# A scan's constant operand moved from SBUF to PSUM bytes, and longer due times for early scatters

## The chip, the cores and the metric

One core of a Trainium2 chip runs the whole program in one launch. The metric is the device time of an execution in microseconds; the kernel before was run three times and its median is 836.9 us. One more execution was profiled, and all rows below come from that one.

## The reference

Three layers run one after the other. The first is a linear attention with a decaying state (4 batches, 8 heads, 768 steps, 48 channels a head), the second sends each of the 3072 tokens to one of 8 experts, the third is a dense layer with a smooth gate.

```python
for t in range(S):                                   # attention, S = 768
    cur = np.einsum('bhd,bhe->bhde', u[None] * kt, vt)
    y[:, :, t] = np.einsum('bhd,bhde->bhe', rt, state + cur)
    state = wt[:, :, :, None] * state + np.einsum('bhd,bhe->bhde', kt, vt)
...
expert_idx = np.argmax(logits, axis=1)               # router, N = 3072, E = 8
for e in range(E):                                   # experts, F = 1024
    mask = expert_idx == e
    h = np.maximum(x[mask] @ w1[e], 0.0)
    out[mask] = gate_w[mask, None] * (h @ w2[e])
...
h = x @ w_in                                         # dense layer, 384 -> 2048 -> 384
sp = np.where(h > 20.0, h, np.log1p(np.exp(np.minimum(h, 20.0))))
out = (h * np.tanh(sp)) @ w_out
```

## The kernel before, in words

The attention is cut into 12 chunks of 64 steps. For a chunk `s`, `scaled` turns the decays `w` into running products inside the chunk. Sixteen sequences (4 batches by 4 pairs of heads) lie behind one another in a row of 16 x 65 = 1040 numbers, the two heads of a pair on the two halves of the partitions. VectorE makes two scans along that row. The first writes `pre`: it multiplies its running value by `w` and adds `once`, a constant that is 1 at the head of each sequence and 0 elsewhere, so that each sequence starts anew. The second runs backwards over the same `w`, with `anew` (the reciprocals of the chunk's whole products) as what is added, and writes `suf`. `kh` is `k` times `suf`, on VectorE; `rh` is `r` times `pre`, on GpSimd (POOL), two halves each.

From these TensorE makes the scores of the chunk (`scores`, L515), the transposed keys and the state that goes to the next chunk (`carried`, L547, L556, L559), and the outputs (`outputs`, L579, L584). POOL masks half of the scores (`affine_select`, L530). Each chunk gives two tiles of 128 tokens. `Router.tile` transposes a tile (L308) and multiplies it with the expert vectors (logits, L313). Tiles are decided in groups of 6, 6, 4, 4, 2 and 2 (`ROUTED`): `decide` finds the expert, ranks the tokens by a product of a triangle with the one-hot rows (`rank`, L360 to L364), and works out each token's row (`desti`, L375). `send` then lets POOL scatter each tile's rows to the experts' lists in HBM with an indirect DMA (L388). The first expert's rows are read back only when all 24 scatters have landed; then come the experts and the dense layer, which are not planned but written out in order.

PSUM has eight banks of 512 fp32 words a partition. Bank 0 (`g.bank`) is kept for the router: logits and ranks of the groups with at least three tiles, the even groups from word 0, the odd ones from word 192, and two words at 460 for a final check (L663). The other seven are handed out by the plan.

The order of the attention's work on each engine is not that of the code. Each step is entered into a `Plan` with an engine, an assumed duration, and what it reads and writes. `order` walks through the steps in simulated time: it takes the engine whose step can start first, and among that engine's steps that could start within 0.02 us of it the one with the longest `way` to the end. That walk fixes the order of instructions on every engine; the real waits are semaphores, which the framework puts in from the buffers that instructions touch.

```python
way[o.n] = o.us + max([self.wait(o, S[q]) + way[q] for q in out[o.n]] + [o.late])
...
t = max(t, at.get(o.eng, 0.0), at.get("port", 0.0) if o.port else 0.0)
...
t, n = min([c for c in can if S[c[1]].eng == eng and c[0] <= t0 + SLACK], key=lambda c: (-way[c[1]], c[1]))
```

Steps marked `port` exclude one another in the plan, whichever engine they are on. Before the change these are both scans, `kh`, and most POOL steps; the POOL steps that only prepare constants at the start are not marked. `late` is a floor for the way that follows a step: 6 us for each chunk still to come, plus 40, for the scores, the same plus 20 for the copies of the outputs, and a flat 7 (`LATE_S`) for a scatter.

Of the kernel before, what the change touches and what calls it, by code (L numbers as in the profile page):

```python
# [10 lines left out]
F32 = mybir.dt.float32  # L11
F32R = mybir.dt.float32r
BF16 = mybir.dt.bfloat16
I32 = mybir.dt.int32
AF = mybir.ActivationFunctionType
ALU = mybir.AluOpType
# [11 lines left out]
NT = N // 128  # L28
XW = DM + 1
KC = DM // 128  # L30
E, F = 8, 1024
# [6 lines left out]
NW, NR, NK, NV, NX = 2, 2, 3, 3, 12  # L38
# [3 lines left out]
SLACK, LATE_S, LATE_F, LATE_O, LATE_A = 0.02, 7.0, 0.0, 20.0, 40.0  # L42
COLS = [slice(0, 64), slice(64, 128)]
REST = 100
SEG = C + 1
NB = B * NP
WIDE = NB * SEG
# [13 lines left out]
class Plan:  # L61
# [13 lines left out]
    def add(self, eng, us, fn, reads=(), writes=(), wake=None, late=0.0, port=None):  # L75
        o = SimpleNamespace(eng=eng, us=us, fn=fn, wake=self.WAKE[eng] if wake is None else wake, need=set(),
                            late=late, port=eng == "pool" if port is None else port, n=len(self.steps), ps=[k for k in {*reads, *writes} if k[0] == "ps"])
        for k in reads:
            if k in self.writer:
                o.need.add(self.writer[k].n)  # L80
        for k in writes:
            o.need.update(p.n for p in self.readers.pop(k, []))
            if k in self.writer:
                o.need.add(self.writer[k].n)
        for k in reads:
            self.readers.setdefault(k, []).append(o)
        for k in writes:
            self.writer[k] = o
        for k in o.ps:
            self.users.setdefault(k, []).append(o)  # L90
        o.need.discard(o.n)
        self.steps.append(o)
        for k in o.ps:

            u = self.users[k][0]
            u.need.update(p for p in o.need if p < u.n)
        return o
# [94 lines left out]
def setup(g, tmp, plan, then):  # L192
# [3 lines left out]
    t = lambda nm, shape, dt=F32: const.tile(shape, dt, name=nm)  # L196
    g.tri, g.ones = t("tri16", [128, 128], BF16), t("ones", [128, 128], BF16)
    g.tiny = t("tiny", [128, 1])
    add("dve", 0.06, lambda: nc.vector.memset(g.tiny, 1e-30), then, ["tiny"])
    g.iota, g.tok = t("iota", [128, NT, E]), t("tok", [128, NT], I32)  # L200
    g.ebase, g.runs = t("ebase", [128, E]), t("runs", [128, len(ROUTED) + 1, E])
    g.oh, g.dest, g.desti = t("oh", [128, NT, E], BF16), t("dest", [128, NT]), t("desti", [128, NT], I32)
    g.posi, g.ids, g.offi = t("posi", [128, NT], I32), t("ids", [128, NT], I32), t("offi", [128, E], I32)
    g.cnt, g.offs_f = t("cnt", [128, E]), t("offs_f", [128, E])
    g.flag, g.flagi = t("flag", [128, 3]), t("flagi", [128, 3], I32)
    g.enT = t("enT", [128, KC, E])
    g.xs = g.dram.tile([E * N, XW], F32, name="xs")
    g.idc = g.dram.tile([N, 1], I32, name="idc")
    ones_f, tri = tmp.tile([128, 128], F32, name="ones_f"), tmp.tile([128, 128], F32, name="tri")
    io = tmp.tile([128, NT, E], I32, name="io")  # L210
    v, p = nc.vector, nc.gpsimd
# [55 lines left out]
def apart(g, key, dma):  # L267

    g.tc.declare_no_dep(dma.ins, group=key, reason="rows of their own")
    g.tc.add_to_no_dep_group(key, dma.ins)  # L270
    g.scatters.setdefault(key, []).append(dma.ins)
# [9 lines left out]
class Router:  # L281
# [44 lines left out]
    def sums(self, qi, G):  # L326

        def at(lo, hi):
            if G < 3:
                return self.plan.bank["ps", "lg", qi][:, lo:hi]  # L330
            return self.g.bank[:, 192 * (qi % 2) + lo:192 * (qi % 2) + hi]
        lg = lambda: at(0, G * E).rearrange("p (t e) -> p t e", e=E)
        rt = lambda: at(64, 64 + (G + 1) * E).rearrange("p (t e) -> p t e", e=E)
        return lg, rt

    def decide(self, qi, j0, G):
# [49 lines left out]
    def send(self, qi, j):  # L386
        g, nc, add = self.g, self.g.nc, self.plan.add
        add("pool", 1.27, lambda: apart(g, "xs", nc.gpsimd.indirect_dma_start(  # L388
            out=g.xs[:, :], out_offset=bass.IndirectOffsetOnAxis(ap=g.desti[:, j:j + 1], axis=0),
            in_=self.xs[:, j % NX], in_offset=None, bounds_check=E * N - 1, oob_is_err=False)),  # L390
            [("x", j % NX), ("gt", j % NX), ("desti", qi), "slots"], [("sent", j)], wake=2.4, late=LATE_S)

    def finish(self):

# [36 lines left out]
def attention(g, ctx):  # L431
# [6 lines left out]
    add = plan.add  # L438
    ring, early = [ctx.enter_context(tc.tile_pool(name=n, bufs=1, side=sd)) for n, sd in (("at0", "left"), ("at1", "right"))]
    v, p, a, pe = nc.vector, nc.gpsimd, nc.scalar, nc.tensor  # L440
    X = ring.tile([128, NX, XW], F32, name="x")
    router = Router(g, ring, plan, ROUTED, X)
    t = lambda nm, shape, n: [ring.tile(shape, F32, name=f"{nm}{i}") for i in range(n)]
# [7 lines left out]
    t = lambda nm, shape, n: [early.tile(shape, F32, name=f"{nm}{i}") for i in range(n)]  # L451
# [2 lines left out]
    PRE, SUF = t("pre", [128, WIDE], 2), t("suf", [128, WIDE + 2], 2)  # L454
    ANEW, junk = t("anew", [128, WIDE + 1], 1)[0], t("junk", [128, NB, C], 1)[0]
    zs = t("zs", [REST, XW], 1)[0]
    once = t("once", [128, WIDE], 1)[0]
    halves = [slice(NB // 2 * i, NB // 2 * (i + 1)) for i in range(2)]
    ROW = [slice(0, 64), slice(64, 128)]
    late = lambda s: TICK * (NCH - s)  # L460
# [16 lines left out]
    def tokens(x, at):  # L477

        return x[:, at:at + WIDE].rearrange("p (n t) -> p n t", t=SEG)[:, :, :C]

    def scaled(s):

        n, nw, nr, nk = s % 2, s % NW, s % NR, s % NK
        w, kw = W[nw], [("w", nw)]
        add("act", 1.36, lambda: a.activation(
            junk, w[:, :WIDE].rearrange("p (n t) -> p n t", t=SEG)[:, :, 1:], AF.Square, bias=bias, accum_out=viol[:, s:s + 1]),
            kw + ["bias"], ["viol"])
        add("dve", 2.31, lambda: v.tensor_tensor_scan(PRE[n], w[:, :WIDE], once, 0.0, ALU.mult, ALU.add),
            kw + ["once"], [("pre", n)], port=True)
        add("dve", 0.25, lambda: v.reciprocal(ANEW[:, SEG::SEG], PRE[n][:, C::SEG]), [("pre", n)], ["anew"])  # L490
        add("act", 0.2, lambda: a.copy(OWN[:, s], PRE[n][:, C::SEG]), [("pre", n)], [("own", s)])
        add("dve", 2.31, lambda: v.tensor_tensor_scan(SUF[n][:, WIDE::-1], w[:, ::-1], ANEW[:, ::-1], 0.0, ALU.mult, ALU.add),
            kw + ["anew"], [("suf", n)], port=True)
        for i, c in enumerate(halves):
            for nm, x, y, z, at, eng in (("r", R, PRE, RH, 0, p), ("k", K, SUF, KH, 2, v)):
                add("dve" if eng is v else "pool", 0.68 if eng is v else 1.19,
                    lambda x=x, y=y, z=z, at=at, c=c, eng=eng: eng.tensor_tensor(z[nk][:, c], x[nr][:, c], tokens(y[n], at)[:, c], op=ALU.mult),
                    [(nm, nr), ("suf" if at else "pre", n)], [(nm + "h", nk, i)], port=True)
# [98 lines left out]


    load("w", 0)
    add("dve", 0.93, lambda: v.memset(once, 0.0), [], ["once"])  # L600
    add("dve", 0.07, lambda: v.memset(once[:, 0::SEG], 1.0), [], ["once"])
    add("pool", 0.95, lambda: p.memset(R[0], 0.0), [], [("r", 0)], port=False)
    add("dve", 0.93, lambda: v.memset(K[0], 0.0), [], [("k", 0)])
    add("pool", 0.95, lambda: p.memset(ANEW, 0.0), [], ["anew"], port=False)
# [20 lines left out]
    for s in range(NCH):  # L625
# [16 lines left out]
        for q in range(2):  # L642
            router.tile(2 * s + q)
    within_range(g, ring, plan, viol, OWN.rearrange("p s n -> p (s n)"))
    router.finish()
    plan.order()


def within_range(g, pool, plan, viol, own):

    nc, add = g.nc, plan.add
    okm = pool.tile([128, 2], F32, name="f_ok")
    ok16 = pool.tile([128, 2], BF16, name="f_ok16")
    ps = g.bank[:, 460:462]
    v = nc.vector
    add("dve", 0.15, lambda: v.tensor_scalar(viol, viol, FAR, None, op0=ALU.is_le), [], ["viol"])
    add("dve", 0.15, lambda: v.tensor_reduce(okm[:, 0:1], viol, axis=AX.X, op=ALU.min), ["viol"], ["ok0"])
    add("dve", 0.3, lambda: v.tensor_tensor(own, own, own, op=ALU.mult), [], [("own", s) for s in range(NCH)])
    add("dve", 0.3, lambda: v.tensor_scalar(own, own, LEAST * LEAST, None, op0=ALU.is_ge), [], [("own", s) for s in range(NCH)])
    add("dve", 0.3, lambda: v.tensor_reduce(okm[:, 1:2], own, axis=AX.X, op=ALU.min), [("own", s) for s in range(NCH)], ["ok1"])  # L660
    add("dve", 0.15, lambda: v.tensor_tensor(ok16, okm[:, 0:1].to_broadcast([128, 2]), okm[:, 1:2].to_broadcast([128, 2]), op=ALU.mult),
        ["ok0", "ok1"], ["ok16"])
    add("pe", 0.1, lambda: nc.tensor.matmul(ps, lhsT=g.ones, rhs=ok16, start=True, stop=True), ["ones", "ok16"], ["okps"])  # L663
    add("dve", 0.15, lambda: v.tensor_scalar(g.flag[:, 0:1], ps[:, 0:1], 127.5, None, op0=ALU.is_lt), ["okps"], ["flag0"])
# [619 lines left out]
```

## Time and profile before

| what | value |
|---|---|
| three runs | 836.5, 836.9, 844.67 us; median 836.9 |
| profiled execution | 835.85 us, span from first to last instruction 834.0 us |
| mean granted TensorE clock | 0.978 |
| busy: TensorE (PE) | 768.0 us, 92% |
| busy: VectorE (DVE) | 649.9 us, 78% |
| busy: ScalarE (ACT) | 486.9 us, 58% |
| busy: GpSimd (POOL) | 410.7 us, 49% |

Busy shares are means over stages of quite different kinds; the attention ends near 171 us and the first expert's products start near 187 us. PEld is TensorE's load of weights, which runs beside its products. An entry in square brackets behind a row is the idle time of the engine just before the row and what ended it.

### The profile page before, as it was taken

How to read it: one execution, taken by the hardware profiler on the slowest of the kernel's cores; microseconds unless marked ns; L12 is line 12 of the kernel's file. 1: busy time of each engine (PE TensorE's matmuls, PEld its weight loads, DVE VectorE, ACT ScalarE, POOL GpSimd, SP SyncE). 2: the span in 40 equal slices, each digit the busy share in tenths (PEclk: the TensorE clock that was granted, in tenths of full speed). 3: DMA queues.
4: the chain of work that ended last, by engine and by line, in shares of the span. 5: the costliest groups of instructions: out<-in, count | busy, mean ns of one | idle time of the engine just before them, and what ended most of it. 6: DMA issues, size and time to landing. Idle time of an engine off the chain costs nothing. (4 is left out here: it accounts for less than half of the span.)

```text
span 834.0 us, 18322 instructions
## 1 busy us (share of the span) xinstructions
PE 768.0 (92%) x7136; PEld 703.7 (84%) x7136; DVE 649.9 (78%) x995; ACT 486.9 (58%) x974; POOL 410.7 (49%) x365
## 2 busy tenths in 40 slices
PE   2579889859999999999999999999999999999993
PEld 2467778748999999999989999999999999999993
DVE  6879879648988988898878777877876876886782
ACT  3546566435566656656556656656656655755651
POOL 8716365546877787766423353334334334334321
PEclk9989999969999999999999999999999999999997
DMA  7765666336767776875200010000001001001001
GB/s 162 193 167 139 165 177 192 122 126 178 182 169 193 208 193 173 202 202 171 59 2 1 1 38 1 1 10 29 1 0 39 1 1 39 0 1 39 1 2 42
DMA packets 62220, 75.50 MB, mean 91 GB/s; under 512 B 9314, under 2 KB 52394, under 8 KB 62122
## 3 DMA queue, kind: packets, MB, share of 16 engines
q1 hardware_dynamic: 58282, 64.75, 29.8%
q0 software_dynamic: 3840, 9.47, 3.2%
q8 instruction: 58, 0.95, 0.5%
q14 instruction: 40, 0.33, 0.1%
HBM read 63.50 MB, written 10.69 MB: 89 GB/s over the span
## 5 line engine op out<-in xcount | busy, mean ns | idle before, releaser
L1085 POOL TENSOR_TENSOR t<-t,t 128x512 f32<-128x512 f32 x94 | 122.0, 1299 | 239.2 <-ACT t L1081 228.0
L1094 DVE TENSOR_TENSOR gl<-t,gh 128x512 fp32r<-128x512 f32 (+1 forms) x97 | 113.6, 1171 | 74.6 <-ACT gh L1091 74.3
L1078 ACT ACTIVATE t<-t,two 128x512 f32<-128x512 f32 (+1 forms) x97 | 69.9, 721 | 118.1 <-DVE t L1075 118.1
L817 PE MATMUL acc<-woh,gl 128*128 128x384 f32 x384 | 129.6, 338 | 0.1
L815 PE MATMUL acc<-woh,gh 128*128 128x384 f32 x384 | 129.3, 337 | 0.0
L816 PE MATMUL acc<-wol,gh 128*128 128x384 f32 x384 | 129.0, 336 | 0.0
L886 POOL TENSOR_TENSOR w0l<-r,w0h 128x384 fp32r<-128x384 f32 x63 | 67.6, 1072 | 60.5 <-ACT w0h L885 49.5
L810 PE MATMUL ph<-xl,wih 128*128 128x512 f32 x240 | 95.0, 396 | 0.0
L809 PE MATMUL ph<-xh,wil 128*128 128x512 f32 x240 | 94.8, 395 | 0.0
L808 PE MATMUL ph<-xh,wih 128*128 128x512 f32 x240 | 93.3, 389 | 0.0
L815 PEld LDWEIGHTS acc<-woh,gh 128*128 128x128 f32 x384 | 72.2, 188 | 4.2
L816 PEld LDWEIGHTS acc<-wol,gh 128*128 128x128 f32 x384 | 72.1, 188 | 4.0
L886 POOL TENSOR_TENSOR w1l<-r,w1h 128x384 fp32r<-128x384 f32 x63 | 71.4, 1134 | 4.4 <-ACT w1h L885 4.1
L817 PEld LDWEIGHTS acc<-woh,gl 128*128 128x128 f32 x384 | 72.0, 188 | 0.4 <-DVE gl L1094 0.4
L1088 DVE TENSOR_TENSOR t<-t,ph 128x512 f32<-128x512 f32 (+1 forms) x97 | 64.9, 669 | 5.8 <-POOL t L1085 5.7
L810 PE MATMUL acc<-hl,w1h 128*128 128x420 f32 x192 | 68.0, 354 | 1.3 <-DVE hl L964 1.3
L808 PE MATMUL acc<-hh,w1h 128*128 128x420 f32 x192 | 69.1, 360 | 0.0
L1091 ACT CAST gh<-t 128x512 fp32r<-128x512 f32 (+1 forms) x97 | 58.9, 607 | 16.9 <-DVE t L1088 16.6
L1068 DVE TENSOR_SCALAR t<-ph 128x512 f32<-128x512 f32 (+1 forms) x97 | 65.4, 675 | 3.4 <-PE ph L810 3.1
L1075 DVE SCALAR_TENSOR_TENSOR t<-t 128x512 f32<-128x512 f32 (+1 forms) x97 | 66.2, 683 | 2.1 <-ACT t L1071 2.1
L809 PE MATMUL acc<-hh,w1l 128*128 128x420 f32 x192 | 67.6, 352 | 0.0
L808 PE MATMUL ph<-xh,w0h 128*128 128x420 f32 x189 | 66.7, 353 | 0.0
(201 smaller groups left out, 1808.3 us busy)
## 6 DMA issues: line engine op xcount, KB each, us to landing
r<-in_moe_w SPq DMA_DIRECT2D x128, 192.0 KB, 3.7
w<-in_w_t SPq DMA_DIRECT2D x12, 520.5 KB, 4.4
d<-in_moe_w_in SPq DMA_DIRECT2D x16, 384.0 KB, 4.0
d<-in_moe_w_out SPq DMA_DIRECT2D x16, 384.0 KB, 4.8
xr<-xs SPq DMA_DIRECT2D x32, 157.9 KB, 4.9
r<-in_r_t SPq DMA_DIRECT2D x24, 192.0 KB, 4.8
k<-in_k_t SPq DMA_DIRECT2D x24, 192.0 KB, 3.8
v<-in_v_t SPq DMA_DIRECT2D x24, 192.0 KB, 3.8
```

What stands on the lines that cost most here:

```text
L808: mm(out, lhsT=wh, rhs=xh, start=start, stop=False)
L809: mm(out, lhsT=wl, rhs=xh, start=False, stop=False)
L810: mm(out, lhsT=wh, rhs=xl, start=False, stop=stop)
L815: mm(out, lhsT=ah, rhs=bh, start=start, stop=False)
L816: mm(out, lhsT=ah, rhs=bl, start=False, stop=False)
L817: mm(out, lhsT=al, rhs=bh, start=False, stop=stop)
L886: (eng or nc.gpsimd).tensor_tensor(lo, r, f32(hi), op=ALU.subtract)
L1068: nc.vector.tensor_scalar(tile_of(i, "t0", mt, bufs=3)[:, q], S[i]["ph"][:, q], 20.0, None, op0=ALU.min)
L1075: nc.vector.scalar_tensor_tensor(t0, t0, 2.0, t0, op0=ALU.add, op1=ALU.mult)
L1078: nc.scalar.activation(tile_of(i, "t1", mt)[:, q], S[i]["t0"][:, q], AF.Ln, bias=g.two)
L1085: (nc.gpsimd if i < TI - 2 else nc.vector).tensor_tensor(t0, t0, S[i]["t1"][:, q], op=ALU.mult)
L1094: nc.vector.tensor_tensor(tile_of(i, "gl", ghl, F32R)[:, q], S[i]["t0"][:, q], f32(S[i]["gh"][:, q]), op=ALU.subtract)
```

## The change

The constant `once` is no longer a row of 1040 fp32 numbers in SBUF. It becomes 1040 bytes in 260 words of PSUM bank 0, from word 212, written at the start as one memset of zeros over the words and four memsets that put a 1 into the right byte of every 65th word. The `pre` scan reads these bytes as its added operand, and its step is no longer marked `port`. To make room, the router's areas in bank 0 move together (104 words a group, ranks from word 48), and the final check's two words go to 208. In the plan the scatter of tile `j` gets a `late` of 7 + 1.3 x (23 - j).

```diff
-            return self.g.bank[:, 192 * (qi % 2) + lo:192 * (qi % 2) + hi]
+            return self.g.bank[:, 104 * (qi % 2) + lo:104 * (qi % 2) + hi]
...
-        rt = lambda: at(64, 64 + (G + 1) * E).rearrange("p (t e) -> p t e", e=E)
+        rt = lambda: at(48, 48 + (G + 1) * E).rearrange("p (t e) -> p t e", e=E)
...
-            [("x", j % NX), ("gt", j % NX), ("desti", qi), "slots"], [("sent", j)], wake=2.4, late=LATE_S)
+            [("x", j % NX), ("gt", j % NX), ("desti", qi), "slots"], [("sent", j)], wake=2.4, late=LATE_S + 1.3 * (NT - 1 - j))
...
-    once = t("once", [128, WIDE], 1)[0]
+    once = g.bank[:, 212:212 + WIDE // 4].bitcast(U8)
...
         add("dve", 2.31, lambda: v.tensor_tensor_scan(PRE[n], w[:, :WIDE], once, 0.0, ALU.mult, ALU.add),
-            kw + ["once"], [("pre", n)], port=True)
+            kw + ["once"], [("pre", n)])
...
-    add("dve", 0.93, lambda: v.memset(once, 0.0), [], ["once"])
-    add("dve", 0.07, lambda: v.memset(once[:, 0::SEG], 1.0), [], ["once"])
+    words = g.bank[:, 212:212 + WIDE // 4].bitcast(I32)
+    add("dve", 0.4, lambda: v.memset(words, 0), [], ["once"])
+    for i in range(4):
+        add("dve", 0.07, lambda i=i: v.memset(words[:, i * (SEG // 4)::SEG], 1 << 8 * i), [], ["once"])
...
-    ps = g.bank[:, 460:462]
+    ps = g.bank[:, 208:210]
```

## Rows read from the trace of the kernel before

**Rows 1.** Busy time by stage: stretch, length, then busy time (instructions) of PE, PEld, DVE, ACT, POOL; clock, DMA.
```profile
13.40:50.00 36.60, 22.45 (x541) 18.93 (x545) 23.93 (x35) 18.51 (x44) 22.34 (x22) 0.95 0.59 152
50.00:171.20 121.20, 105.62 (x3328) 89.51 (x3319) 99.08 (x213) 71.33 (x189) 60.11 (x53) 0.96 0.58 161
...
190.00:834.00 644.00, 628.80 (x3244) 585.45 (x3243) 506.48 (x696) 389.31 (x726) 308.12 (x266) 0.99 0.26 70
```

**Rows 2.** What PE waited for up to 190 us: total us, times, longest us.
```profile
PE bank L547 <- POOL ident masks.py:199: 13.4, 1, 13.4
PE bank L515 <- issue: 10.0, 8, 2.7
...
PE bank L547 <- DVE kh L497: 6.0, 2, 3.7
```

**Rows 3.** Timeline of the attention's end.
```profile
167.96 0.97 POOL L388 DMA_INDIRECT xs<-x,desti  x1 [2.44 <-DVE r_d L348]
...
172.11 0.16 DVE L375 CAST desti<-dest 128x2 int32<-128x2 f32 x1
...
177.20 0.98 POOL L388 DMA_INDIRECT xs<-x,desti  x1 [0.31 <-issue]
...
183.01 1.31 PE L942 MATMUL tr<-ident,xr 105*128 105x105 f32 x6 [6.04 <-ACT xr L800]
```

**Rows 4.** Timeline of the first 20 us: start us, us, engine, line, work.
```profile
3.62 0.23 POOL L610 TENSOR_SCALAR_AFFINE_SELECT same<-same 64x64 f32<-64x64 f32 x1
...
4.54 1.15 ACT L485 ACTIVATE junk<-w,bias 128x1024 f32<-128x1024 f32 x1 [2.43 <-DMA w<-in_w_t]
4.55 2.32 DVE L488 TENSOR_TENSOR_SCAN pre<-w,once 128x1040 f32<-128x1040 f32 x1
4.71 2.20 POOL L612 TENSOR_SCALAR_AFFINE_SELECT after<-after 64x64 f32<-64x64 f32 x1
...
7.27 2.33 DVE L492 TENSOR_TENSOR_SCAN suf<-w,anew 128x1041 f32<-128x1041 f32 x1
7.64 2.00 POOL L610 TENSOR_SCALAR_AFFINE_SELECT same<-same 64x64 f32<-64x64 f32 x1
...
12.02 1.36 POOL masks.py:199 TENSOR_SCALAR_AFFINE_SELECT ident<-ident 128x128 f32<-128x128 f32 x1
...
15.80 2.31 POOL L497 TENSOR_TENSOR rh<-r,pre 128x512 f32<-128x512 f32 x2
...
17.03 2.27 PE L515 MATMUL bank<-rh,kh 64*64 64x64 f32 x64 [1.63 <-POOL rh L497]
...
19.41 0.73 DVE L526 COPY_PREDICATED at<-after,bank 128x512 f32<-128x512 int32 x1 [6.11 <-PE bank L515]
```

**Rows 5.** Timeline, two places where DVE and POOL overlap.
```profile
93.20 0.72 DVE L526 COPY_PREDICATED at<-after,bank 128x512 f32<-128x512 int32 x1
93.25 1.38 POOL L530 TENSOR_SCALAR_AFFINE_SELECT at<-at 64x512 f32<-64x512 f32 x2 [0.73 <-ACT at L528]
...
100.04 2.32 DVE L488 TENSOR_TENSOR_SCAN pre<-w,once 128x1040 f32<-128x1040 f32 x1
...
101.05 2.27 POOL L388 DMA_INDIRECT xs<-x,desti  x1 [6.42 <-DVE desti L375]
```

**Rows 6.** The line of the first scan: ns min/median/max.
```profile
L488 DVE TENSOR_TENSOR_SCAN pre<-w,once x12: 2298/2322/2764, 4.6 to 137.2; 128x1040 f32<-128x1040 f32 x12
```

**Rows 7.** DVE groups by line: shapes, count, busy us, mean ns, idle before them.
```profile
L488 DVE TENSOR_TENSOR_SCAN pre<-w,once 128x1040 f32<-128x1040 f32 x12 | 29.0, 2420 | 0.2
...
L565 DVE TENSOR_TENSOR state<-bank,own 128x384 f32<-128x384 f32 x22 | 11.2, 537 | 5.2 <-PE bank L559 5.2
...
L371 DVE TENSOR_TENSOR runs<-runs,bank 128x8 f32<-128x8 f32 x6 | 0.9, 158 | 3.3 <-PE bank L313 2.2 <-PE bank L663 0.8 <-PE bank L364 0.3
...
L886 DVE TENSOR_TENSOR w0l<-r,w0h 128x384 fp32r<-128x384 f32 x1 | 0.6, 558 | 0.0
```

**Rows 8.** Timeline, a first scan with logits beside it.
```profile
64.29 2.76 DVE L488 TENSOR_TENSOR_SCAN pre<-w,once 128x1040 f32<-128x1040 f32 x1
...
65.45 0.52 PE L313 MATMUL bank<-enT,r_xT 128*64 128x8 f32 x12
```

More of the change, by code (lines that the diff above doesn't have):

```diff
@@ L13 @@
 BF16 = mybir.dt.bfloat16
+U8 = mybir.dt.uint8
 I32 = mybir.dt.int32
```

## The prediction, made before the changed kernel was run

> **What bounds the kernel now.** I read the slices of busy time first, then the busy time by stage, then what PE waits for, and last the timeline of the stretches that the change can touch. The reader should see three different kernels. From 190 us on, PE is busy 628.8 of 644 us [rows 1]: experts and dense layer are bound by TensorE, nothing of the change runs there, and whatever is gained or lost before shifts that part as a whole. Between 50 and 171 us PE is busy 105.6 of 121.2 us, DVE 99.1, POOL 60.1 [rows 1]. Most of PE's 15.6 us of idle time there is no wait for DVE or POOL: the row "issue" of the scores has 10.0 us in 8 pieces [rows 2], which no operand explains. So the steady part is nearly at TensorE's pace. The start is the slack part: between 13.4 and 50 us PE is busy 22.5 of 36.6 us [rows 1], it waits 13.4 us for POOL to make the identity and 6.0 us for `kh` [rows 2]. The end is the other: PE waits 6.0 us before the experts' first transposes [rows 3], behind the last scatter and the read of the experts' rows.
>
> **The scan and POOL.** What the change can remove is a block between two engines. A 64x64 select takes POOL 0.23 us; the same form started at 4.71, inside the first scan of 4.55 to 6.87, takes 2.20 and ends with it [rows 4]. A scatter started inside a `pre` scan takes 2.27 us and ends 0.96 after the scan, where others take 0.97 [rows 3, 5]. Where DVE takes one operand from PSUM there is no such thing: two selects of 64x512 beside a predicated copy from a bank take 0.69 each [rows 5]. So I take it that `pre` with a PSUM operand leaves POOL alone, while `suf` and `kh`, with two SBUF operands, block it as before.
>
> [...]
>
> **Start, step by step.** POOL's eight instructions from 4.71 to 13.38 follow one another with 0.1 us of idle time at most. The select of 4.71 gives back 2.20 - 0.23 = 1.97 us. The next select, at 7.64 for 2.00 us, then starts near 5.7, still beside the scan that no longer blocks, and gives back 1.77 more. The identity's select, now 12.02 to 13.38, falls into the first `suf` scan (7.27 to 9.60) and ends with it, near 9.7. So it comes 3.7 us earlier, and with it what follows on POOL: the three memsets of `v` (2.3 us), and `rh`, now from 15.80 and then from 12.0; its first half, 1.2 us later, releases the scores, now at 17.03 [rows 4]. These release the copy at 19.41, before which DVE sat idle 6.11 us [rows 4]; its queue, and the loads that wait for buffers, go along. I count -3.8 us, at least 0 (loads fill the gap), at most -3.8 for this chain.
>
> **Middle.** The 12 scans have a mean of 2.420 us against a median of 2.322 [rows 6, 7]: three were themselves held by POOL, 1.2 us in all. DVE is busy 82% there and PE 87%, so I count a third, -0.4 us (0 to -1.2). Three scatters and a few selects blocked by `pre` come free sooner; POOL is half idle, so 0.
>
> **The operand's own price.** No row has a byte operand. From both sides by the spread of this scan, 2.298 to 2.764 us [rows 6]: -0.3 to +5.3 us over 12. I take 0, because the nearest pair of rows, 128x384 with one operand from a bank (0.537 us) and with two from SBUF (0.558), shows no surcharge [rows 7], and 2.32 us for 1040 elements is the pace of a recurrence. [...]
>
> **The memsets** at the start (one of 1040 elements out, one of 260 and four small ones in) cost nothing while the load of the first `w` covers them: ACT's first reader waits for it until 4.54 and the scan starts at 4.55 [rows 4]. Without that cover the balance would be about -0.3 us, by the 0.93 and 0.07 us of the plan.
>
> **The longer way of scatters.** By the code a scatter's way was 1.27 + 7 = 8.3; now tile 12 has 22.6, tile 16 has 17.4, tile 22 has 9.6. For tiles 0 to 11 it changes nothing, because their `x` buffer is used again six chunks later and that path is already longer (30 for tile 10 against a new 25). On POOL the rivals, `rh` and the selects, keep longer ways. What moves is the queue before the scatter: turns, logits and ranks of tiles 12 to 23 on PE, decisions on DVE, now ahead of their peers but still behind the outputs, whose way is at least 29. At the end eight scatters stand back to back from 167.96, and the last starts at 177.20, though its `desti` is there at 172.27 [rows 3]. Were POOL free then, the last two would start at 172.3 and 173.6: 3.6 us. I count half, -1.8 (0 to -3.6); what is late next is `desti` itself.
>
> **The wait that is added.** `once` shares bank 0 with logits and ranks. The sum over ranks in L371 waited 2.2 us for a logits product and 0.8 us for L663, both of which write other columns of that bank [rows 7]. So the framework orders all accesses to a bank: a logits product behind a `pre` scan in the order must wait for the scan's end, and behind it stands all of PE's queue; a scan behind logits must wait for PE, and behind it stand `anew`, `suf` and `kh`. The plan doesn't know this, since the keys differ. In today's order one such pair overlaps from 51 us on: logits at 65.45 inside the scan of 64.29 to 67.05, 1.6 us [rows 8]. I count +1.6, from 0 to eight scans of 2.32, 18.6.
>
> **Sum.** -3.8 - 0.4 + 0 - 1.8 + 1.6 = -4.4 us on an execution of 835.85 us (its span of 834.0 and 1.85 around it), so 831.45. The median of the runs is 836.9, 1.05 higher; on that scale 832.5 us, and rivals are given on it too.
>
> **Rivals.** (1) The freed port lets the plan fill DVE's hole. In the plan both scans exclude POOL's `rh`; with `pre` out of that, the second `suf` can be placed before the copy at 19.41, into the 6.1 us of idle time. Then PE's 6.0 us of waits for `kh` go as well: 832.5 - 6.1 = 826.4. For it: PE idles 14 us between 13.4 and 50 [rows 1]. Against: a `suf` there blocks `rh`, which gates the scores. (2) Nothing is gained, or the change doesn't do what it says: bytes from PSUM still block POOL, or the start is held by loads in SP's order and PE's issue gaps, so that PE catches up to the same pace: 837. For it: PE at 87% in the middle. (3) Slower: the bank. If the new order sets logits behind scans, PE stops for up to 2.32 us each time in the stage where it is the bound. Break-even is the gain of 6.0 over 2.32, or 2.6 full waits; five give 11.6 - 6.0 = +5.6, 842.5 us. For it: L371's waits. Against: today one overlap in eight scans.
>
> **How the numbers follow.** Forecast 0.50, (1) 0.20, (2) 0.18, (3) 0.12. About 1%, 8.4 us, is what a measurement here can tell from no change: faster below 828.5, slower above 845.3. Faster gets most of (1) and the forecast's lower edge, 0.24; slower takes half of (3), 0.06; the same 0.70. The forecast alone spans 829 to 836, by its terms' ends. The range reaches to (1) below and into (3) above: 825.5 to 840.5 leaves out about 2 in 10.
>
> **What would show it.** In the changed kernel: POOL's selects near 5 us at 0.23, the identity near 9.7, `rh` before 13 and the scores near 13; `pre` scans at 2.32 with no long POOL partner; the last scatter's start less than 4 us after its `desti`; rows of PE waiting for L488, or of L488 waiting for L313, for the bank. I am wrong if the order changes more than I think: the plan is a chain of close choices, and one product placed elsewhere moves a stage's end by microseconds.

## The result, and the profile of the changed kernel

The changed kernel took 828.5 us (median of four runs, 827.76 to 830.04) beside 837.77 us for the kernel before (four runs): a ratio of 0.988 with a 95% interval of 0.984 to 0.992. The forecast was 832.5 us, -4.4 us; measured were -9.3 us (8.4 below the 836.9 us from which it was made). The time lies inside the range (825.5 to 840.5). The profiled execution has a span of 826.0 us, 8.0 less than before.

Busy time by stage in the changed kernel, in the columns of [rows 1]: the end of the start, the steady part to the last outputs, and the experts with the dense layer.

```profile
13.40:50.00 36.60, 24.99 (x823) 20.86 (x823) 32.09 (x39) 23.47 (x59) 17.88 (x22) 0.91 0.74 170
50.00:163.20 113.20, 97.84 (x3019) 83.39 (x3011) 88.72 (x194) 64.02 (x169) 49.66 (x49) 0.94 0.61 168
...
182.00:826.00 644.00, 628.83 (x3245) 585.48 (x3243) 506.12 (x696) 389.27 (x726) 307.65 (x266) 0.99 0.27 70
```

The last line is the last line of [rows 1] moved by 8 us: nothing in the experts or the dense layer changed, the whole gain lies ahead of 182 us. In the start PE went through 823 products where it had 541 before. Its waits, answering [rows 2]:

```profile
PE bank L548 <- DVE kh L498: 17.4, 3, 11.1
PE bank L516 <- issue: 9.9, 7, 2.3
PE tr L945 <- ACT xr L803: 3.5, 1, 3.5
...
PE bank L361 <- DVE pre L489: 1.1, 1, 1.1
```

The 13.4 us of waiting for the identity are gone; the first wait is now 11.1 us, for `kh`. (Lines of the changed kernel are one or three higher than before: the scan is L489, the scores L516, the scatter L389.) The timeline of the start, answering [rows 4]:

```profile
4.70 0.23 POOL L615 TENSOR_SCALAR_AFFINE_SELECT after<-after 64x64 f32<-64x64 f32 x1
...
5.06 2.32 DVE L489 TENSOR_TENSOR_SCAN pre<-w,bank 128x1040 f32<-128x1040 f32 x1 [0.96 <-DMA w<-in_w_t]
5.66 0.24 POOL L613 TENSOR_SCALAR_AFFINE_SELECT same<-same 64x64 f32<-64x64 f32 x1
...
7.76 0.29 POOL masks.py:199 TENSOR_SCALAR_AFFINE_SELECT ident<-ident 128x128 f32<-128x128 f32 x1
7.77 2.46 DVE L493 TENSOR_TENSOR_SCAN suf<-w,anew 128x1041 f32<-128x1041 f32 x1
...
10.47 3.12 POOL L498 TENSOR_TENSOR rh<-r,pre 128x512 f32<-128x512 f32 x2
...
13.65 1.60 PE L516 MATMUL bank<-rh,kh 64*64 64x64 f32 x64
...
15.38 2.31 DVE L493 TENSOR_TENSOR_SCAN suf<-w,anew 128x1041 f32<-128x1041 f32 x1
...
17.61 0.70 DVE L527 COPY_PREDICATED at<-after,bank 128x512 f32<-128x512 int32 x1
```

The select of 5.66 lies inside the scan and takes 0.24 us; before, the select inside this scan took 2.20. The scores start at 13.65 instead of 17.03. And the plan has set the second `suf` scan (15.38) ahead of the copy (17.61); before, DVE stood idle there for 6.11 us. The outputs of the first chunk are copied out of PSUM at 29.81 us, before at 34.84; those of the fourth at 62.68 against 75.99 would be a lead of 13 us, but of the last at 160.44 against 165.99: the lead swings, and 5.6 us of it reach the end of the attention. The end, answering [rows 3]:

```profile
166.12 0.17 DVE L376 CAST desti<-dest 128x2 int32<-128x2 f32 x1
...
169.02 1.02 POOL L389 DMA_INDIRECT xs<-x,desti  x1 [0.30 <-issue]
...
175.10 1.31 PE L945 MATMUL tr<-ident,xr 105*128 105x105 f32 x6 [3.46 <-ACT xr L803]
```

The last `desti` is 6.0 us earlier than before. The last scatter follows it by 2.90 us (before 5.09), which makes 8.2, and 7.9 of these are still there at the experts' first transposes.

### The profile page after: what moved, and what is told of

It is laid out like the page before. It is cut to its first block, busy times and chain, and to the rows that moved or that the text cites. A ratio compares the mean times of both kernels' runs of the same rounds, so it can differ in the third digit from the quotient of the medians.

```text
span 826.0 us, 18303 instructions
## 1 busy us (share of the span) xinstructions
PE 766.0 (93%) x7136; PEld 702.0 (85%) x7136; DVE 648.3 (78%) x998; ACT 486.3 (59%) x974; POOL 394.9 (48%) x365
```

## The experiments

The change has three parts that can be set one by one: the operand (bytes in PSUM or floats in SBUF), the mark in the plan (the scan excludes POOL or not), and the scatters' way. Without the mark the plan gives another order of instructions on every engine; without the way, another order on PE, VectorE and ScalarE, and on POOL only where the mark is off too. The operand alone doesn't change the order, since the plan only sees names. All of them keep the router's areas in bank 0 where the changed kernel has them. Where floats stood, the constant was written by one memset and four small ones, so that the plan had the same steps.

```diff
# floats instead of bytes
-    once = g.bank[:, 212:212 + WIDE // 4].bitcast(U8)
+    once = t("once", [128, WIDE], 1)[0]
# the mark as before
-            kw + ["once"], [("pre", n)])
+            kw + ["once"], [("pre", n)], port=True)
# the way as before; steeper
-... late=LATE_S + 1.3 * (NT - 1 - j))
+... late=LATE_S)
+... late=LATE_S + 2.6 * (NT - 1 - j))
```

The runs were made in three groups, each on one chip with runs of the kernel before between them. That kernel took 848.07 us (median of 31) in the first group, 839.26 (24) in the second and 848.15 (29) in the third, on three different chips. All ratios are to it within a group; they are not quotients of the two medians, and differ from these by up to 0.0017. From the experts' first transposes to the end of the span all fourteen traces take 650.2 to 652.6 us, so that kernels and chips differ only in what lies ahead of these.

**First group: each part alone, and the two without the bytes.**

> The order of before on every engine; only the scan's constant is read as bytes from PSUM (the five memsets of the changed kernel with it). Theory A (the prediction's start term): POOL is no longer held by the first scan, the selects near 5 us take 0.23, the identity ends near 9.7 instead of 13.4, and the span falls by about 4 us, to 830 on the profile's scale (834.0 before). Theory B (the gain is the plan's new order, the second suf scan placed ahead of the first copy): without that order the start stays within 1.5 us of before, span 832.5 to 834.5. Rival C (the bank): PE waits for the scan or the scan for PE at more than one place, and the span is 834 or more.

> The scan stays on an SBUF operand, but the plan is told that it leaves POOL alone (port mark taken off), so the order is that of the changed kernel but for the scatters' way. Theory A: the block is still there, POOL's selects near 5 us take 2.2, nothing is gained at the start, span 833 to 835. Theory B: the order alone, with the second suf scan ahead of the first copy, brings the steady part 4 to 5.5 us earlier; span 829 to 830.

> Only the scatters' longer way, with the SBUF operand and the port mark of before. The prediction's tail term: last scatter 1.8 us (0 to 3.6) earlier against its desti, span 832. By the trace of the changed kernel, where the last scatter starts 2.7 us after its desti instead of 4.9: span 2.2 us shorter, 831.8. Rival: turns, logits and ranks moved ahead disturb the attention and eat the gain: 834 or more.

> The changed kernel's order on every engine, with the scan's constant as 1040 floats in SBUF. Theory A: without the freed POOL the 4 us at the start are lost again: span 830 against 826.0 of the changed kernel. Theory B: the order carries the gain; span within 1 us of 826, or below it, since the wait for bank 0 (1.1 us once) is gone too.

| kernel | median, us | ratio | 95% interval |
|---|---|---|---|
| bytes alone | 848.33 | 1.0018 | 0.9991 to 1.0044 |
| mark alone | 850.86 | 1.0036 | 1.0009 to 1.0063 |
| way alone | 847.07 | 0.9989 | 0.9966 to 1.0012 |
| mark and way, floats | 849.92 | 1.0023 | 0.9995 to 1.0051 |

No part alone gained, and the mark and the way with floats together gained nothing either. Theory B failed on this chip: the mark's order with floats is 2.8 us slower than before. The way alone shortens the stretch from the last `desti` to the last scatter as forecast (2.92 us, 5.09 before), but nothing of that can be told in the time. Expectations of absolute spans (830, 834) could not be read here, since this chip is 10 us slower. For the bytes alone, theory A's mechanism shows in the trace and no gain can be told from the times: the first outputs come at 32.2 us (34.84 in the first trace of before, 36.07 in the one below), and the outputs that before has at 97.65 and 97.97 come at 91.94. At the next chunk the lead is gone: 113.65, before 112.23 and 113.51. Busy time by stretch and the wait of PE in between:

```profile
92.00:100.00 8.00, 4.91 (x199) 3.84 (x201) 7.71 (x16) 4.36 (x13) 3.44 (x4) 1.00 0.68 200
100.00:111.00 11.00, 10.58 (x124) 7.92 (x115) 1.06 (x3) 5.12 (x12) 6.24 (x7) 0.54 0.39 114
111.00:114.00 3.00, 3.00 (x120) 2.92 (x119) 2.53 (x8) 0.35 (x1) 0.00 (x0) 1.00 0.18 66
...
99.47 1.00 PE L516 MATMUL bank<-rh,kh 64*64 64x64 f32 x33 [3.09 <-issue]
```

PE stood 3.09 us without a product, and then the granted clock was 0.54 for 11 us: PE is busy 10.58 of 11 us, and from 100 to 110 us each stretch of 2 us has a clock of 0.50. Before has its own wait there (1.94 us) and a clock of 1.00 behind it in the trace of the second group:

```profile
104.64 0.82 PE L515 MATMUL bank<-rh,kh 64*64 64x64 f32 x33 [1.94 <-issue]
...
106.00:111.00 5.00, 4.92 (x104) 3.84 (x105) 0.63 (x3) 4.44 (x12) 4.03 (x5) 1.00 0.75 213
```

This does not show that the low clock took the gain. Both traces of before are from faster chips, and against the second of them the bytes lead again at the eighth outputs (127.28, before 130.97) and at the eleventh (162.08 and 165.09); only at the last are they behind (174.53 and 170.64). What before does at that place on a chip like this one was not traced.

**Second group: the whole, and two parts of three.**

> The changed kernel as it is, on the chip of these runs, where the kernel before takes about 848 us rather than 837. Theory D (the parts need one another: the new order pays only with a scan that leaves POOL alone): 0.988 of before again, since each part alone gave 0.999 to 1.004 and order and way without the bytes 1.002. Rival E (the gain hangs on where TensorE's clock falls, which differs by chip): 0.995 to 1.003 here.

> Bytes in PSUM and the mark taken off, scatters with the flat way of before. Theory D: the order of the attention is nearly that of the changed kernel; only the tail term of about 2 us goes, 0.990 to 0.991 of before. Rival (the longer way carries more, by the order it gives the router's work): 0.995 or more.

> Bytes in PSUM and the scatters' longer way, with the plan still told that the scan excludes POOL. Theory D: without the new order no more than the two parts alone, 1.0018 and 0.9989, so 0.998 to 1.003 of before. Rival (bytes pay with any order, and the way pays at the tail): 0.993 or less.

> The kernel before, unchanged, for its profile on the chip of these runs: ratio 0.998 to 1.002. Against its first profile (span 834.0) it shows which stretches are longer here: by rival E the ones with a low granted clock, between 100 and 190 us; by theory D all stretches alike.

| kernel | median, us | ratio | 95% interval |
|---|---|---|---|
| changed kernel | 830.2 | 0.9900 | 0.9862 to 0.9937 |
| bytes and mark | 832.79 | 0.9940 | 0.9911 to 0.9969 |
| bytes and way | 834.26 | 0.9944 | 0.9922 to 0.9966 |
| before | 840.24 | 1.0012 | 0.9981 to 1.0043 |

The gain repeats, as theory D had it for the whole. For the parts it is off: bytes with either of the other two give about 0.6%, more than it allowed for bytes and way (0.998 to 1.003) and less than for bytes and mark (0.990). This chip is one of the faster ones, so that rival E could not be decided here. On it the bytes pay in the order of before too: with the way, which shortens nothing at the end there (4.19 us from the last `desti` to the last scatter, 4.05 and 3.94 in the two traces of bytes alone), they gain 5.0 us. Floats in the new order were not run on a chip like this one, so how the 9.1 us divide between the operand and the order is not shown. Between the changed kernel and the one without the longer way there are 2.6 us of medians, but the intervals overlap, and the traces warn against giving them to the way. The order on PE is the same in both up to the logits that the changed kernel runs near 130 us; yet the outputs ahead of these stand, in the changed kernel and in the one without the way, at

```profile
126.53 0.86 ACT L595 COPY x<-bank 128x384 f32<-128x384 f32 x2
```
```profile
130.67 0.86 ACT L595 COPY x<-bank 128x384 f32<-128x384 f32 x2
```

4.1 us apart before any engine's order on this path differs. Single traces differ by that much. What the way itself does stands at the end: the last scatter starts 2.90 us after the last `desti` with it (167.15 to 170.05) and 4.23 without (170.21 to 174.44), 1.3 us.

**Third group: the operand at equal order, and a steeper way.**

> The changed kernel's order with floats in SBUF, a second time, now beside the changed kernel itself. In the trace of its first run the identity ended at 13.5 instead of 9.5, the first copy stood at 21.60 instead of 17.57, and a POOL product beside the second-chunk scan took 4.33 us for two instead of 2.30. Theory A (bytes carry the gain by what POOL no longer waits for, 4 to 5 us at the start): 0.995 to 1.003 of before, at least 4 us above the changed kernel. Theory B (the order carries it): within 1.5 us of the changed kernel.

> Bytes alone in the order of before, a second time. In its first trace the first outputs were copied at 32.2 instead of 34.8 to 36.1, and the lead of 3 to 6 us held to 92 us and was lost by 114 in a stretch in which the granted clock was 0.50. Theory A on a chip whose clock holds there: 0.995 to 0.997 of before. Rival E (the lead is always given back in low clock): 0.999 to 1.002.

> The changed kernel beside the two runs above. If the kernel before takes 836 to 841 us on this chip: 0.988 to 0.991. If it takes about 848 (the chip of the first four runs): by theory A with rival E, 0.990 to 1.000, and in any case 4 us or more below the same order with floats.

> The changed kernel with twice the slope in the scatters' way (7 + 2.6 us for each later tile), so that the router's work of tiles 0 to 11 is moved ahead as well. By the prediction's account of the way (the last scatters find POOL free) the queue of scatters at the end is shorter still, last scatter 2 us after its desti instead of 2.8: 1 us below the changed kernel. Rival (router work ahead of its need disturbs the attention while it fills): 1 to 4 us above it.

| kernel | median, us | ratio | 95% interval |
|---|---|---|---|
| mark and way, floats | 850.0 | 1.0031 | 1.0009 to 1.0054 |
| bytes alone | 846.75 | 0.9982 | 0.9951 to 1.0013 |
| changed kernel | 846.34 | 0.9983 | 0.9961 to 1.0004 |
| changed, steeper way | 841.83 | 0.9915 | 0.9882 to 0.9948 |

The first and third line have the same order on every engine; only the operand differs. It is worth 850.0 - 846.34 = 3.7 us by the medians (4.1 by the means), about the 4 us that theory A asked for; theory B, within 1.5 us of the changed kernel, is out on this chip. The start with floats:

```profile
4.71 2.12 POOL L615 TENSOR_SCALAR_AFFINE_SELECT after<-after 64x64 f32<-64x64 f32 x1
...
15.89 2.28 PE L516 MATMUL bank<-rh,kh 64*64 64x64 f32 x64 [1.63 <-POOL rh L498]
...
20.45 4.33 POOL L498 TENSOR_TENSOR rh<-r,pre 128x512 f32<-128x512 f32 x2
20.90 2.90 DVE L489 TENSOR_TENSOR_SCAN pre<-w,once 128x1040 f32<-128x1040 f32 x1
...
32.96 0.87 ACT L595 COPY x<-bank 128x384 f32<-128x384 f32 x2 [0.74 <-PE bank L585]
```

and with bytes:

```profile
4.70 0.23 POOL L615 TENSOR_SCALAR_AFFINE_SELECT after<-after 64x64 f32<-64x64 f32 x1
...
13.50 2.27 PE L516 MATMUL bank<-rh,kh 64*64 64x64 f32 x64 [0.93 <-POOL rh L498]
...
18.05 2.30 POOL L498 TENSOR_TENSOR rh<-r,pre 128x512 f32<-128x512 f32 x2
18.50 2.30 DVE L489 TENSOR_TENSOR_SCAN pre<-w,bank 128x1040 f32<-128x1040 f32 x1
...
29.70 0.87 ACT L595 COPY x<-bank 128x384 f32<-128x384 f32 x2 [0.73 <-PE bank L585]
```

With the mark off, the plan lays `rh` beside the scan. With floats each holds the other: 4.33 and 2.90 us; with bytes 2.30 and 2.30. The lead of 3.3 us at the first outputs is 3.3 us at the experts' first transposes as well, with floats and with bytes at

```profile
196.71 1.14 PE L945 MATMUL tr<-ident,xr 105*128 105x105 f32 x6 [3.45 <-ACT xr L803]
```
```profile
193.43 1.31 PE L945 MATMUL tr<-ident,xr 105*128 105x105 f32 x6 [4.38 <-ACT xr L803]
```

though it doesn't stay so in between: at the eighth chunk's outputs it is 6.0 us (123.22 and 117.19). POOL is busy 418.9 us with floats and 398.8 with bytes.

Against before, however, the changed kernel gains only 1.8 us on this chip, inside what rival E gave for a chip like it (0.995 to 1.003) and far from the 0.988 to 0.990 of the faster ones. Its interval (0.9961 to 1.0004) does not exclude that it gains nothing. The bytes alone, at 0.9982, lie between what theory A and rival E expected, and decide nothing. The steeper way gains 4.5 us more, and its interval doesn't touch that of the changed kernel: it is faster than both expectations had it, on the one chip on which it ran. Its last scatter starts 2.23 us after its `desti` instead of 2.93, a gain of 0.7 where 0.8 was expected; the other 3.8 us are not explained by that.

```profile
179.82 0.17 DVE L376 CAST desti<-dest 128x2 int32<-128x2 f32 x1
...
182.05 1.21 POOL L389 DMA_INDIRECT xs<-x,desti  x1 [0.30 <-issue]
```

Where the changed kernel loses on this chip, its own traces tell. Its median is 16.1 us above that of the second group, while before loses 8.9 us from one chip to the other. Busy time from 100 us to the experts' first transposes, first in the second group and then in the third:

```profile
100.00:176.11 76.11, 63.53 (x1809) 54.59 (x1801) 54.38 (x167) 38.91 (x107) 37.47 (x37) 0.92 0.53 157
```
```profile
100.00:193.43 93.43, 72.65 (x1837) 62.03 (x1836) 56.44 (x169) 42.47 (x114) 40.79 (x40) 0.85 0.45 132
...
DVE runs L372 <- remote: 5.1, 1, 5.1
DVE r_mx L348 <- remote: 3.9, 1, 3.9
```

Nearly the same products (1809 and 1837) take PE 9.1 us more at a lower clock (0.85 beside 0.92), and its idle time grows from 12.6 to 20.8 us. Two rows of what DVE waited for are new: 9.0 us that end by "remote", which is what the trace says where it sees nothing on this core that ended them. PE stands behind the second of them: it waits 3.9 us for the one-hot rows. Yet both stalls lead back to PE. The instructions that wait so in this trace (L372, L348 and, on ACT, L317) all read banks that PE's products write, and by the record the products had ended well before. The last ones into the bank that L372 reads, ahead of the first stall's end, are logits that ended at 138.48, and the transposes that ACT waits for beside the second ended at 176.85. That is 5.6 and 2.9 us before the waits end:

```profile
137.20 1.28 PE L314 MATMUL bank<-enT,r_xT 128*64 128x8 f32 x36 [0.66 <-ACT r_xT L317]
144.09 0.16 DVE L372 TENSOR_TENSOR runs<-runs,bank 128x8 f32<-128x8 f32 x1 [5.14 <-remote]
...
176.00 0.85 PE L309 MATMUL bank<-ident,x 128*128 128x128 f32 x6 [0.81 <-DVE x L595]
179.77 0.86 ACT L317 COPY r_xT<-bank 128x384 f32<-128x384 f32 x2 [2.55 <-remote]
```

So by the record these waits outlast the products they are for; why they do, no run shows.

## Why the prediction came out as it did

**Start: -3.8 forecast, -3.3 measured at equal order.** The chain went as worked out: selects at 0.23, the identity at 8.05 to 9.84 in the traces with bytes (forecast 9.7), `rh` from 10.5 to 12.3 (before 13), the scores from 13.2 to 13.7 (near 13). At the first outputs the operand alone gives 3.3 us (third group). The profiled execution has 5.0 us there; the floats in the new order stand at 32.96, 1.9 earlier than before, so that the order seems to have a part in it. The 3.7 us by which the runs of the third group differ are more than this term: they hold all that the operand does, for which start, middle and bank were to give 3.8 + 0.4 - 1.6 = 2.6, and in an order that lays `rh` beside a scan. The forecast let the lead run through to the end; it does at equal order (3.3 us at both ends), while the bytes alone in the order of before showed no gain on the slower chips (0.9982 and 1.0018).

**Rival 1: its mechanism came, its price didn't.** The second `suf` went into DVE's hole, as the rival said, but PE still waits 5.9 us for `kh` in the second chunk, and only the identity's wait went. On a slower chip the mark without bytes costs 0.36%, so there the new order doesn't pay with a scan that holds POOL. With bytes it may be worth up to 4.1 us (834.26 against 830.2 in the second group, with intervals that overlap); in the third group, bytes with the mark and the way are no better than bytes alone (846.34 and 846.75). So it lies between 0 and 4 us.

**Middle: -0.4.** The scans that POOL held are gone (their mean fell from 2420 to 2305 ns, 1.4 us in all; what it gave the whole was not measured by itself), as the one line shows, against a median of 2322 and a longest of 2764 ns [rows 6]:

```profile
L489 DVE TENSOR_TENSOR_SCAN pre<-w,bank x12: 2295/2304/2321, 5.1 to 125.0; 128x1040 f32<-128x1040 f32 x12
```

The same line settles **the operand's own price**, taken as 0: with the byte operand from PSUM the scan takes no longer than with floats from SBUF (medians of 2304 and 2322 ns). For the pace of a recurrence the rows have only the two scans, 2.32 us for 1040 elements and 2.33 for 1041 [rows 4]; what sets it, no run shows.

**Scatters' way: -1.8.** The stretch from `desti` to the last scatter shrank by 2.2 us in the profiled pair. By parts: 1.3 us with bytes and mark, 2.2 with floats in the old order (5.09 to 2.92), and nothing with bytes in the old order (3.94 to 4.05 without the way, 4.19 with it). The length of this stretch came out near the forecast for this change, and depends on the order it meets. What it gives the whole is less sure: the way alone gave 0.9989, and the 2.6 us of the second group lie within the noise.

**Scatters beside scans: 0 in the sum.** In the kernel before four of 24 scatters took 2.26 to 2.93 us beside a scan, where others took 0.97; in the changed kernel none does in its first trace (1.27 us at most). Beside a `suf` scan, still with two SBUF operands, a scatter in the third group's changed kernel took 2.84 us and ended 0.8 us after the scan. What in the scatter is held, the trace doesn't tell.

```profile
112.04 2.32 DVE L493 TENSOR_TENSOR_SCAN suf<-w,anew 128x1041 f32<-128x1041 f32 x1
112.33 2.84 POOL L389 DMA_INDIRECT xs<-x,desti  x1 [0.16 <-issue]
```

**The bank's wait: +1.6.** It exists and is smaller. PE's rank product waited once for the scan, which reads the same bank:

```profile
124.98 2.31 DVE L489 TENSOR_TENSOR_SCAN pre<-w,bank 128x1040 f32<-128x1040 f32 x1
...
127.34 0.18 PE L361 MATMUL bank<-oh,tri 128*128 128x48 bf16 x1 [1.07 <-DVE pre L489]
```

1.1 us here, none in the second trace, 0.3 in the third; in these no scan waited for logits. In the other kernels with bytes PE waited 0.8 to 2.0 us for a scan, or not at all, and one scan (bytes and way) 0.4 us for logits: the wait hangs on the order. None comes near the 6.0 us of rival 3, which is out.

**What was off: the size.** In the profiled pair the account closes. The last outputs are 5.6 us earlier where start, middle and bank together were to give 3.8 + 0.4 - 1.6 = 2.6; the router behind them gives 0.4, where nothing was counted; the scatters' queue gives 2.2 instead of 1.8; 0.2 are lost behind it: 8.0 against 4.4. So the term that was mis-sized is the lead that the attention keeps to its end, 5.6 us instead of 2.6. Of the 3.0 us between, 0.5 are the bank's wait (1.1 instead of 1.6) and 1.2 the lead at the first outputs (5.0 instead of 3.8); the other 1.3 arise further on. The new order, which the forecast carried as a rival and not in the sum, is the likeliest source, by the 4.1 us that the mark was worth in the second group; for this pair it is argued and not shown, because floats in the new order did not run on a faster chip. (What is between these 8.0 us and the 9.3 lies between the profiled executions and the medians.)

By its number the result lies nearer to rival 1 (826.4) than to the forecast (832.5), and the range, 15 us wide, would hold the 1.8 us of the third group as well as the 9.3 of the first runs. That the time fell inside it says little for the sum. One row was read too widely, without a price: of the 10.0 us of "issue" before the scores [rows 2], 2.7 lie ahead of 50 us. Between 50 and 171 us they are 7.3, and only with PE's other "issue" rows, 13.0, most of the 15.6.

What the forecast didn't foresee at all is how much the stage behind the start varies. The gain was 9.3 us in the first runs and 9.1 in the second group, but 1.8 in the third. The stalls that end by "remote" and the lower clock are seen there; what causes them is open, and so is why the changed kernel loses more there than before, of which there is no trace from a chip like that. The clock's part is not shown either: from 100 us to the experts' first transposes it is 0.94 and 0.89 in the two traces of before, and 0.85 in this one of the changed kernel.

## What to carry to other kernels

Before a block between two engines is lifted, find the chain that waits behind it: here a quarter-microsecond select that took 2.2 us beside a scan, and with it the identity and the first scores. A planner may be told of a freed resource only when it is free: on a slower chip the mark without the bytes cost 0.36%. Compare parts on one chip: on the faster chip of the second group two of the three parts gave 0.6% and all three 1.0%; on the slower ones the bytes alone and all three together gave 0.2% at most, and only the steeper way 0.85%. A lead at the start counts only as far as the stage behind it holds the pace, so follow it chunk by chunk, and measure on more than one chip.

## What the runs showed of the hardware

- In the third group the scan with floats in SBUF and the product on POOL beside it held each other: two halves of 128x512 took 4.33 us beside the scan with floats and 2.30 beside the one with bytes, and the scan 2.90 and 2.30.
- In the kernel before a memset on POOL was not held: one of 64x768 took 0.73 us inside a scan with two SBUF operands, as another did right behind one.

```profile
6.86 0.73 POOL L621 MEMSET v<- 64x768 f32 x1
...
10.97 2.33 DVE L488 TENSOR_TENSOR_SCAN pre<-w,once 128x1040 f32<-128x1040 f32 x1
11.08 0.73 POOL L621 MEMSET v<- 64x768 f32 x1
```

- The chips differ by about as much as the change is worth: the kernel before took 837 to 839 us in the first runs and the second group, 848 in the first and third. None of the six traces from the former has a DVE stall that ends by "remote"; six of the eight from the latter have them, 3.6 to 9.5 us in each.
- After PE had stood 3.09 us, its granted clock was 0.54 for 11 us in the first group's bytes alone; after 3.24 us at the same place in the second group's bytes and way, 0.84 over the same 11 us.
